# A new written-out order for the first 28 slices of a fused attention and gated-FFN kernel, with one load moved and four copies split

## The chip, the cores and the metric

The kernel runs on one core of a Trainium2 chip. The metric is the device time of one execution in microseconds (us). The kernel before takes 221.94 us, the median of three runs (221.68 to 222.19). The five engines are TensorE (PE in the profile; PEld is its weight loading), VectorE (DVE), ScalarE (ACT), GpSimd (POOL) and SyncE (SP). Each takes its own instructions strictly in the order in which the kernel lists them, and waits for another engine through semaphores.

## The reference

Eight batches, eight heads, 512 tokens and 32 state rows of width 64. Tokens attend to the state and the state attends to the tokens; both results, 8 x 544 rows of 512 numbers, go through a gated feed-forward layer.

```
a      = softmax(scale * x @ state^T)        # tokens over state rows
xread  = a @ state
a2     = softmax(scale * state @ x^T)        # state rows over tokens
sread  = a2 @ x
X      = rows of concat([xread, sread])      # 4352 x 512
out    = (relu(X @ w_gate) * (X @ w_val)) @ w_out     # d_ff = 1536
```

The softmax's subtraction of the maximum and the 1e-9 are not in the kernel, whose inputs keep the scores small.

## The kernel before, in words

All matmul operands are bf16. `xread @ w_gate` is regrouped as `a @ (state @ w_gate)`: for each batch the kernel first makes U, the product of the batch's state with both weight matrices, and then multiplies the transposed attention weights `ans` by U. Work is cut into **slices**: slice (b, jf) is 128 of the 1536 hidden columns of batch b. A step has a short name, and these names are used throughout:

- `gv.b.jf` (L289): four matmuls of 128x512 that make gate and value of a slice in two PSUM banks. `re` (L313) is ScalarE's ReLU of the gate bank, `mu` (L317) VectorE's product of it with the value bank. A bank is free once its reader (`re` for the first of the two banks, `mu` for the second) is done.
- `o.b.i` (L326): four output matmuls, a third of one 128-token block; `of` (L334, `fin_x`) copies a finished block out of PSUM on ScalarE and stores it from SP's queue.
- `c` and `co` (L262, L284): U of batches 0 and 1 in pieces of 128 or 256 columns as the weights arrive, and its copy out of PSUM; `u` and `uo` (L262, L274): the same for later batches, 512 columns at a time.
- `dx`, `dw`, `do`, `ds`: loads of x, of the two first weight matrices, of `wo` and of the state, all issued by GpSimd, one after the other. `xc` and `stc` convert to bf16 what came in as f32.
- `stT`/`sto`, `xT`/`xo`, `aT`/`ao`: transposes on TensorE of the state, of x and of the attention weights, each with its copy out of PSUM; `xd` (L148), `ad` (L197) and `state_T_dma` (L122): the same by a DMA transpose from SP's queue, with `state_out_dma` (L130) as GpSimd's copy of the state into its place.
- `sc`, `ex`, `nr`, `nx`: scores (L170), exponential on ScalarE (L177), row sums and reciprocal (L183, L185) and scaling (L189) on VectorE.
- `xp` (`x_pad`, L224): GpSimd copies x into a padded buffer, of which there are two, taken in turn; `sr` (L232) and `sn` (L241): the state's attention over tokens from that buffer, and its scaling.
- `spin`: a matmul on zeros whose result nobody reads; `on`: a memset of the padding.

The order is set in three parts. First come some direct statements (x of batch 0, the state of batches 0 and 1, the identity, memsets). Then a string, `program`, lists every step of the first 28 slices (batches 0 and 1, and slices 0 to 3 of batch 2) word by word; `@30` behind a step gives the PSUM banks it takes, and `.act`, `.dve` or `.pool` the engine of a copy. The last loop makes the slices from (2, 4) on: in each turn `gv`, `re`, `mu`, one `o` piece that lags by 18 slices, and then the units that `at(b, jf, ...)` hung on this slice: `att_half` (the `sc ex nr nx` of the next batch), `u_block` (three `u` with their copies), `sr`, `x_trans_dma`, `x_pad`, `x_load`. In that loop `bank` deals out the six banks 0 to 5 in turn to `gv`, `sc` and `u`, and 6 and 7 to the `o` blocks.

The scheduler is in manual mode: nothing is reordered between the text and the engines' queues, except that loads of weights run ahead of matmuls on TensorE.

Of the kernel before, what the change touches and what calls it, by code (L numbers as in the profile page):

```python
# [16 lines left out]
def kernel(  # L17
# [9 lines left out]
    nc = tc.nc  # L27

    B, H, S, D = x.shape
# [26 lines left out]
    HK = H // NK  # L56
# [12 lines left out]
    stT = const.tile([128, B, H, 64], BF16, name="stT")  # L69
# [6 lines left out]
    xf, xb, xT, e_sn, a_sn, ANS, U, hsb, sr_sb = {}, {}, {}, {}, {}, {}, {}, {}, {}  # L76
    copy = {"act": nc.scalar.copy, "dve": nc.vector.tensor_copy, "pool": nc.gpsimd.tensor_copy}

    given, turn = [], {"r": 0, "o": 1}

    def bank(name, kind="r"):

        if given:
            n = given.pop(0)
        elif kind == "spare":
            n = 6 + turn["o"] % 2
        else:
            n = turn["r"] % 6 if kind == "r" else 6 + turn["o"] % 2
            turn[kind] += 1
        return psum.tile([128, 512], FP32, name=name, tag=f"b{n}")  # L90

# [22 lines left out]
    def state_T(g):  # L114
        ps = held["st", g] = bank("stT_ps").bitcast(BF16)[:, 0:512]
        for i in range(4):
            nc.tensor.transpose(ps.rearrange("p (q i m) -> p q i m", i=4, m=8)[:, :, i],
                                st_b[:, g % 3, i].rearrange("p h d -> p (h d)"), id128)
# [31 lines left out]
    def x_T(b, lo, n):  # L150

        if b not in xT:
            xT_alloc(b)
        ps = held["xT", b, lo] = bank("xT_ps").bitcast(BF16)[:, 0:128 * n].rearrange("p (k t) -> p k t", t=128)
        for k in range(n):
            nc.tensor.transpose(ps[:, k], x_blocks(b)[:, lo + k], id128)  # L156
# [5 lines left out]
    def att_sc(b, jp):  # L162
        if b not in e_sn:
            e_sn[b] = att.tile([128, 2, NC, NJ * Ns], BF16, name="e_sn", tag="e_sn", bufs=4)
            a_sn[b] = att.tile([128, 2, NC, NJ * Ns], BF16, name="a_sn", tag="a_sn")
        t = held["sc", b, jp] = bank("sc_ps")
        ps = t.rearrange("p (r c j n) -> p r c j n", r=2, c=NC, j=2)
        for h in range(4 * jp, 4 * jp + 4):
            for k in range(2):
                nc.tensor.matmul(ps[:, h % 2, 2 * k:2 * k + 2, h // 2 % 2], xT[b][:, 2 * h + k], stT[:, b, h],  # L170
                                 start=True, stop=True)
# [49 lines left out]
    def x_pad(b):  # L221

        v = xa[:, b % NX].rearrange("p (c h) d -> p h c d", c=NC)[:, :, :, 0:D]
        nc.gpsimd.tensor_copy(out=v, in_=xb[b])  # L224

    def sr_mm(b, kind="r"):

# [170 lines left out]
    def spin(n, cols=512):  # L398
        for i in range(n):
# [6 lines left out]
             "sc": att_sc, "ex": att_exp, "nr": att_sum, "nx": att_scale, "aT2": att_T2, "ao2": att_out2, "aT": att_T, "ao": att_out,  # L406
             "c": c_unit, "co": c_out, "u": u_unit, "uo": u_out, "gv": gv, "re": relu, "mu": mult, "o": out_part,
             "of": fin_x, "xd": x_trans_dma, "ad": att_aT_dma, "xp": x_pad, "sr": sr_mm, "sn": sr_norm}
    program = """
    dx.1.0.2 dx.1.1.2 stc.0.0.act stc.0.1.act xc.0.0.dve dw.0.0.128 spin.7 stT.0@4 xc.0.1.act dw.1.0.128 on xT.0.0.4@2  # L410
    sto.0.0.dve sto.0.1.act xT.0.4.4@5 xo.0.0.4.dve dw.0.128.128 xo.0.4.4.dve dw.1.128.128 spin.1 sc.0.0@3 dw.0.256.256 ex.0.0 xT.0.8.4@0
    xT.0.12.4@1 xo.0.8.4.dve dw.1.256.256 xo.0.12.4.act nr.0.0 spin.2 sc.0.1@6 dw.0.512.256 xT.1.0.8@4 ex.0.1 nx.0.0
    xo.1.0.8.act nr.0.1 dw.1.512.256 spin.2 xT.1.8.8@2 xo.1.8.8.dve sc.1.0@5 dw.0.768.256 ex.1.0 nx.0.1 dw.1.768.256
    spin.2 c.0.0.128@30 sc.1.1@1 co.0.0.128.0.act nr.1.0 aT.0.1@6 co.0.0.128.1.act dw.0.1024.256 aT.0.0@4 ex.1.1
    ao.0.0.dve ao.0.1.act dw.1.1024.256 spin.1 c.0.128.128@25 c.1.0.128@30 nr.1.1 co.0.128.128.1.act gv.0.0@14
    co.0.128.128.0.act co.1.0.128.1.act nx.1.0 re.0.0 dw.0.1280.256 c.1.128.128@65 nx.1.1 gv.0.1@20 co.1.0.128.0.act
    co.1.128.128.0.act mu.0.0 co.1.128.128.1.act aT.1.1@7 re.0.1 dw.1.1280.256 aT.1.0@1 ao.1.1.act c.0.256.256@36
    ao.1.0.dve c.1.256.256@54 mu.0.1 co.0.256.256.0.act gv.1.1@21 dx.2.0.1 co.1.256.256.0.act co.0.256.256.1.dve
    re.1.1 gv.1.0@73 co.1.256.256.1.act mu.1.1 ds re.1.0 c.1.512.256@05 c.0.512.256@62 co.1.512.256.1.dve
    co.1.512.256.0.act gv.1.2@41 co.0.512.256.1.act mu.1.0 do.0.6 co.0.512.256.0.act gv.0.3@70 re.1.2 xp.1 gv.1.5@52  # L420
    re.0.3 mu.1.2 re.1.5 mu.0.3 gv.0.4@36 mu.1.5 re.0.4 xp.0 c.1.768.256@47 c.0.768.256@15 mu.0.4 co.1.768.256.0.act
    gv.0.2@03 co.0.768.256.0.act co.1.768.256.1.dve re.0.2 gv.0.5@26 do.6.12 co.0.768.256.1.act mu.0.2 gv.1.7@41 dx.3.0.1
    re.0.5 re.1.7 mu.0.5 gv.0.7@70 mu.1.7 re.0.7 gv.1.3@53 mu.0.7 re.1.3 gv.1.4@24 mu.1.3 re.1.4 gv.1.6@61 mu.1.4
    re.1.6 c.1.1280.256@70 c.0.1280.256@53 mu.1.6 co.1.1280.256.0.act c.1.1024.256@24 stc.1.0.pool xT.2.0.8@6
    co.0.1280.256.0.act co.1.1024.256.0.dve xT.2.8.8@1 co.0.1280.256.1.act co.1.1024.256.1.dve stc.1.1.pool
    c.0.1024.256@75 xo.2.8.8.act gv.0.10@23 co.1.1280.256.1.dve stc.3.1.pool co.0.1024.256.1.dve re.0.10 gv.1.9@40
    co.0.1024.256.0.act xo.2.0.8.dve stc.2.0.pool re.1.9 gv.0.6@12 mu.0.10 stc.3.0.pool re.0.6 mu.1.9 gv.0.11@57 mu.0.6
    stc.2.1.pool re.0.11 gv.0.8@64 mu.0.11 re.0.8 stT.1@3 gv.1.10@10 mu.0.8 sto.1.0.act sto.1.1.dve re.1.10 sc.2.0@2 o.0.0@7 ex.2.0
    mu.1.10 nr.2.0 sc.2.1@5 gv.0.9@34 ex.2.1 re.0.9 nx.2.0 o.0.1 mu.0.9 gv.1.11@12 nr.2.1 xd.3 re.1.11 o.0.2 mu.1.11
    o.0.3@6 nx.2.1 ad.2 of.0.0.act u.2.0.1024@05 u.2.1.512@34 uo.2.0.1024.0.dve uo.2.0.1024.1.act sr.0@1 sr.1@2  # L430
    uo.2.1.512.1.act sn.0 u.2.0.0@50 sn.1 xp.2 xp.3 o.0.4 uo.2.0.0.0.act uo.2.0.0.1.dve uo.2.1.512.0.dve
    o.0.5 o.0.6@7 of.0.1.act u.2.1.0@12 u.2.0.512@50 uo.2.1.0.0.act uo.2.1.0.1.dve u.2.1.1024@34 o.0.7
    uo.2.1.1024.0.act uo.2.1.1024.1.dve uo.2.0.512.0.act gv.1.8@12 uo.2.0.512.1.dve re.1.8 o.0.8 mu.1.8
    o.0.9@6 of.0.2.act gv.2.0@45 re.2.0 gv.2.2@01 mu.2.0 re.2.2 gv.2.1@23 mu.2.2 re.2.1 gv.2.3@45 mu.2.1
    re.2.3 mu.2.3
    """
    for word in program.split():
        word, _, banks = word.partition("@")
# [8 lines left out]
    def at(b, jf, f, *args):  # L447
        units.setdefault(NF * b + jf, []).append(lambda: f(*args))
# [20 lines left out]
        sr_norm(b)  # L469

    first, lag = 2 * NF + 4, 18
    at(2, 6, x_load, 4, 0, 1)
    for g in (2, 3):
        at(2, 2 + g, state_T_dma, g)
        at(2, 8 + g, state_out_dma, g, 0, "pool")
        at(2, 8 + g, state_out_dma, g, 1, "pool")
    for b in range(3, B):
        s = b - 1
        for i, jf in enumerate((4, 5) if b == 3 else (3, 4)):
            at(s, jf, att_half, b, i)  # L480
        for part, jf in enumerate((7, 10)):
            at(s, jf, u_block, b, part)
            paired.add(NF * s + jf)
        if b + 1 < B:
            at(s, 9, x_trans_dma, b + 1)
            at(s, 9, x_pad, b + 1)
        if b + 2 < B:
            at(s, 10, x_load, b + 2, 0, 1)
# [7 lines left out]
    for g in range(first, NF * (B + 1)):  # L496
        b, jf = divmod(g, NF)
# [47 lines left out]
```

## Time and profile before

| what | value |
|---|---|
| median of 3 runs | 221.94 us (221.68 to 222.19) |
| the profiled execution, its own time | 222.66 us |
| its span, from the first to the last instruction | 220.9 us |
| mean granted TensorE clock | 0.999 |
| busy: PE, DVE, ACT, POOL | 214.6, 130.8, 123.5, 40.6 us |
| gv (L289) and o (L326) matmuls | 94.1 and 94.6 us busy |
| GpSimd's idle time ahead of the padding copies (L224) | 69.2 us, of it 52.2 for `sr` on TensorE |

A busy PE in the page is not a PE at its peak, because the ends of pipelined matmuls are modelled; the start of each instruction says more. In the second part of the page each digit is a fortieth of the span (5.5 us). The timeline view gives for each engine the start of an instruction (or of a run of equal ones), its length, the number behind `x`, and in brackets the idle time just before it with the instruction or transfer that ended it.

### The profile page before, as it was taken

To read this page: it belongs to the slowest core of one execution; us is meant where nothing else is said; L and a number is where in the kernel's file an instruction comes from. 1 tells how busy PE (TensorE), PEld (TensorE's weight loads), DVE (VectorE), ACT (ScalarE), POOL (GpSimd) and SP (SyncE) were. 2 spreads that over 40 slices of the span, in tenths; PEclk is the share of its full clock that TensorE was granted. 3 is DMA by queue.
4 is the path that set the end of the run, shared out by engine and by line. 5 is a ranking of instruction groups with operands and counts; after the bars stand their busy time and mean duration, and the time that the engine had idled before them with its cause. 6 is when DMAs were issued, how large, how long until landed. Compare 5 with 4: busy or idle time off the path is not lost.

```text
span 220.9 us, 4858 instructions
## 1 busy us (share of the span) xinstructions
PE 214.6 (97%) x1955; PEld 105.2 (48%) x1955; DVE 130.8 (59%) x229; ACT 123.5 (56%) x236; POOL 40.6 (18%) x51
## 2 busy tenths in 40 slices
PE   7899999999999999999999999999999999999994
PEld 2553454444544444444444444445454445666543
DVE  5796898865787567664766487648665334222100
ACT  4699887465666565555566555646654543223221
POOL 7875830080035400040003000000000000000000
PEclk9999999999999999999999999999999999999999
DMA  7999999579057993655353105501411122222132
GB/s 165 165 195 197 198 241 204 52 213 167 8 127 112 185 142 98 142 96 103 85 130 83 50 19 142 121 16 43 112 37 53 47 47 50 50 57 85 50 95 96
DMA packets 42215, 23.65 MB, mean 107 GB/s; under 512 B 22640, under 2 KB 37872, under 8 KB 42192
## 3 DMA queue, kind: packets, MB, share of 16 engines
q0 software_dynamic: 16896, 9.05, 30.4%
q1 hardware_dynamic: 24400, 13.54, 24.3%
q10 hardware_dynamic: 896, 0.75, 1.4%
q8 instruction: 15, 0.25, 0.5%
q14 instruction: 8, 0.07, 0.1%
HBM read 18.35 MB, written 8.91 MB: 123 GB/s over the span
## 4 chain that ended last, share of the span: by engine, by line
PE 89%; DMA 7%; issue 1%; DVE 1%; POOL 1%; POOLq 0%
PE o_ps L326 39%; PE gv_ps L289 36%; PE gv_ps L306 5%; PE up L262 4%; DMA wv_sb<-in_moe_w_val_dram 4%; DMA xb<-in_x_dram 3%; PE sc_ps L170 1%; PE sr_ps L232 1%; PE o_ps L355 1%; PE upc L262 1%; PE xT_ps L156 0%; POOL xb L394 0%; DVE h_sb L317 0%; DVE stT L134 0%; POOL id masks.py:199 0%
## 5 line engine op out<-in xcount | busy, mean ns | idle before, releaser
L326 PE MATMUL o_ps<-wo_sb,h_sb 128*128 128x512 bf16 x372 | 94.6, 380 | 0.0
L289 PE MATMUL gv_ps<-ans,U 128*128 128x512 bf16 x384 | 94.1, 380 | 0.0
L317 DVE TENSOR_TENSOR h_sb<-gv_ps,g_sb 128x512 bf16<-128x512 f32 x96 | 65.3, 689 | 45.2 <-ACT g_sb L313 44.1
L313 ACT ACTIVATE g_sb<-gv_ps 128x512 bf16<-128x512 f32 (+1 forms) x108 | 63.0, 586 | 44.9 <-PE gv_ps L289 33.8
L289 PEld LDWEIGHTS <-U 128*128 128x128 bf16 x384 | 36.3, 98 | 42.2 <-issue 0.4
L326 PEld LDWEIGHTS <-h_sb 128*128 128x128 bf16 x372 | 35.3, 98 | 40.8 <-issue 2.1
L224 POOL COPY xa<-xb 128x2048 bf16<-128x2048 bf16 x8 | 15.1, 1898 | 69.2 <-PE sr_ps L232 52.2
L334 ACT COPY o_sb<-o_ps 128x512 f32<-128x512 f32 x31 | 18.3, 590 | 16.8 <-PE o_ps L326 14.8
L274 DVE CAST U<-up 128x512 bf16<-128x512 f32 x36 | 22.7, 685 | 5.7 <-PE up L262 5.6
L274 ACT CAST U<-up 128x512 bf16<-128x512 f32 x36 | 18.9, 594 | 12.1 <-PE up L262 12.0
L177 ACT ACTIVATE e_sn<-sc_ps 128x512 bf16<-128x512 f32 x16 | 9.6, 599 | 10.6 <-PE sc_ps L170 10.6
L317 DVE TENSOR_TENSOR hs_sb<-gv_ps,g_sb 128x256 bf16<-128x256 f32 x12 | 5.1, 425 | 15.1 <-PE gv_ps L306 9.2
L183 DVE TENSOR_REDUCE cs<-e_sn 128x16 f32<-128x512 bf16 x16 | 10.9, 681 | 4.4 <-ACT e_sn L177 4.4
L189 DVE TENSOR_TENSOR a_sn<-e_sn,rc 128x512 bf16<-128x512 bf16 x16 | 10.9, 686 | 0.4
L262 PEld LDWEIGHTS <-stT 64*32 64x32 bf16 x560 | 6.3, 90 | 9.6 <-issue 8.3
L284 ACT CAST U<-upc 128x512 bf16<-128x512 f32 (+1 forms) x21 | 10.0, 551 | 1.1 <-PE upc L262 1.1
L170 PEld LDWEIGHTS <-xT 128*128 128x128 bf16 x128 | 5.8, 98 | 4.4 <-issue 0.9
L262 PE MATMUL up<-wg_sb,stT 64*32 64x512 bf16 (+1 forms) x168 | 7.3, 349 | 0.0
L262 PE MATMUL up<-wv_sb,stT 64*32 64x512 bf16 (+1 forms) x168 | 7.3, 349 | 0.0
L170 PE MATMUL sc_ps<-stT,xT 128*128 128x64 bf16 x128 | 6.7, 193 | 0.5 <-DVE stT L134 0.3
L306 PE MATMUL gv_ps<-br,wg_sb 128*128 128x256 bf16 x48 | 7.2, 273 | 0.0
L306 PE MATMUL gv_ps<-br,wv_sb 128*128 128x256 bf16 x48 | 7.2, 273 | 0.0
(54 smaller groups left out, 112.9 us busy)
## 6 DMA issues: line engine op xcount, KB each, us to landing
out_dram<-o_sb SPq DMA_DIRECT2D x26, 256.0 KB, 2.4
xb<-in_x_dram POOLq DMA_DIRECT2D x6, 512.0 KB, 7.1
wo_sb<-in_moe_w_out_dram POOLq DMA_DIRECT2D x2, 768.0 KB, 13.5
out_dram<-o_sb SPq DMA_DIRECT2D x11, 128.0 KB, 2.4
wg_sb<-in_moe_w_gate_dram POOLq DMA_DIRECT2D x5, 256.0 KB, 9.4
wv_sb<-in_moe_w_val_dram POOLq DMA_DIRECT2D x5, 256.0 KB, 10.0
xb<-in_x_dram POOLq DMA_DIRECT2D x3, 256.0 KB, 5.9
st_f<-in_state_dram POOLq DMA_DIRECT2D x1, 384.0 KB, 11.5
```

Source lines behind the costliest of these rows:

```text
L170: nc.tensor.matmul(ps[:, h % 2, 2 * k:2 * k + 2, h // 2 % 2], xT[b][:, 2 * h + k], stT[:, b, h], start=True, stop=True)
L183: nc.vector.reduce_sum(out=cs, in_=e_v, axis=AX.X)
L189: {"dve": nc.vector, "pool": nc.gpsimd}[eng].tensor_tensor(out=by_pair(a_sn[b], jp).rearrange("p r (j n) -> p r j n", n=Ns), in0=e_v, in1= ...
L224: nc.gpsimd.tensor_copy(out=v, in_=xb[b])
L262: nc.tensor.matmul(dst[parity][32 * j:32 * j + 32], stT[r:r + 64, b, 2 * j + parity, 32 * parity:32 * parity + 32], wsb[r:r + 64, j, lo:lo ...
L274: copy[eng](out=U[b][:, w, kc, lo:lo + 512], in_=held["u", b, w, lo][kc])
L289: nc.tensor.matmul(ps[w], U[b][:, w, kc, f0:f0 + 128], ANS[b][:, kc].rearrange("p c t -> p (c t)"), start=(kc == 0), stop=(kc == NK - 1))
L306: nc.tensor.matmul(ps[w][:, 0:nt], wsb[:, j, f0:f0 + 128], br[:, j].rearrange("p b n -> p (b n)"), start=(j == 0), stop=(j == NJ - 1))
L313: nc.scalar.activation(out=g_sb[:, 0:n], in_=ps[0][:, 0:n], func=AF.Relu)
L317: nc.vector.tensor_tensor(out=dst, in0=ps[1][:, 0:n], in1=held["g", b, jf][:, 0:n], op=ALU.mult)
L326: nc.tensor.matmul(held["o", b, tsub], src[:, jf, tsub * 128:(tsub + 1) * 128], wo_sb[:, jf], start=(jf == 0), stop=(jf == NF - 1))
L334: copy[eng](out=o_sb, in_=held["o", b, tsub])
```

## The change

1. The `program` string is another list. Steps, engines of the copies and banks are chosen anew; all steps that compute something appear as before. There are 18 `spin` matmuls in place of 15. The state comes ahead of x at the start, `sc.1.0` comes behind both transposes of x of batch 1, `gv.0.0` comes behind four `c` units in place of three; x of batch 3 is loaded behind a cast of the state, and `xp.3` stands before `xp.2`. The list ends otherwise: `gv.2.1 gv.2.3 gv.2.0`, three `o`, then `gv.2.2`, and the `re` and `mu` of three of the four slices behind it.
2. `bank` deals out banks 1, 0, 4, 2, 3, 5 in the last loop in place of 0 to 5, and begins the `o` banks with the other one.
3. `x_pad` makes two copies of four heads each in place of one of eight.
4. x of batch 4 is loaded at slice (2, 5) behind `state_out_dma` of state group 2 (batches 4 and 5), which moves from slice (2, 10) to (2, 5); it was at (2, 6), with nothing of the state ahead of it. The copies for group 3 stay at (2, 11).

```diff
-    given, turn = [], {"r": 0, "o": 1}
+    given, turn = [], {"r": 0, "o": 0}
...
-            n = turn["r"] % 6 if kind == "r" else 6 + turn["o"] % 2
+            n = (1, 0, 4, 2, 3, 5)[turn["r"] % 6] if kind == "r" else 6 + turn["o"] % 2
...
-        nc.gpsimd.tensor_copy(out=v, in_=xb[b])
+        for hs in (slice(0, HK), slice(HK, H)):
+            nc.gpsimd.tensor_copy(out=v[:, hs], in_=xb[b][:, hs])
...
     program = """
...
+    stc.0.0.dve stc.0.1.act spin.7 stT.0@0 sto.0.1.dve dx.1.0.2 dx.1.1.2 dw.0.0.128 xc.0.1.dve dw.1.0.128
+    dw.0.128.128 dw.1.128.128 dw.0.256.256 dw.1.256.256 dw.0.512.256 dw.1.512.256 dw.0.768.256 dw.1.768.256
+    dw.0.1024.256 dw.1.1024.256 dw.0.1280.256 dw.1.1280.256 dx.2.0.1 ds xc.0.0.act on xp.0 xT.0.0.4@1 do.0.6
+    xT.0.4.4@2 sto.0.0.act xo.0.0.4.dve xo.0.4.4.act spin.3 sc.0.0@3 xT.0.8.4@4 xT.0.12.4@5 ex.0.0 xo.0.12.4.act
+    xo.0.8.4.dve nr.0.0 spin.3 sc.0.1@6 xT.1.0.8@0 xT.1.8.8@1 ex.0.1 nx.0.0 xo.1.0.8.act spin.2 sc.1.0@2
+    c.1.0.128@34 c.0.0.128@56 nr.0.1 xo.1.8.8.dve spin.1 sc.1.1@0 nx.0.1 ex.1.0 co.0.0.128.0.act aT.0.1@1 aT.0.0@2
+    ex.1.1 co.1.0.128.0.act ao.0.0.act c.1.128.128@50 spin.2 c.0.128.128@32 nr.1.0 co.0.0.128.1.act
+    co.0.128.128.0.act co.0.128.128.1.act ao.0.1.dve gv.0.0@16 co.1.128.128.1.act re.0.0 xp.1 co.1.0.128.1.act
...
+    c.1.256.256@57 co.0.256.256.1.act ao.1.1.dve co.1.256.256.0.dve mu.0.1 mu.0.0 co.1.256.256.1.act gv.1.1@20
...
+    mu.0.3 gv.1.5@20 stc.1.0.pool mu.1.0 mu.0.2 re.1.5 gv.0.5@34 re.0.5 mu.1.5 c.0.768.256@67 c.1.768.256@52 mu.0.5
+    stc.1.1.pool stc.2.0.pool c.0.1024.256@13 do.6.12 co.0.768.256.0.act co.1.768.256.0.dve gv.0.4@04
...
+    co.1.1280.256.1.dve co.0.1280.256.0.act re.1.6 co.1.1024.256.1.act re.0.7 gv.1.11@42 stT.1@1 xT.2.0.8@0
+    gv.0.9@35 sto.1.0.dve xo.2.0.8.dve mu.0.7 mu.1.6 sto.1.1.act re.1.11 re.0.9 xT.2.8.8@1 gv.1.10@40 re.1.10
...
+    mu.1.9 mu.1.8 nr.2.1 nx.2.1 o.0.5 u.2.1.512@10 u.2.1.0@54 u.2.0.0@23 uo.2.1.512.1.act o.0.1 uo.2.1.0.0.dve
+    uo.2.1.512.0.dve uo.2.0.0.1.dve ad.2 of.0.1.act o.0.2 u.2.0.1024@06 uo.2.0.0.0.act uo.2.1.0.1.act u.2.1.1024@52
+    u.2.0.512@14 of.0.0.act sr.1@3 sr.0@7 uo.2.0.1024.1.dve sn.1 sn.0 uo.2.0.512.1.dve uo.2.0.512.0.act o.0.6@6
+    uo.2.1.1024.1.dve stc.3.0.pool dx.3.0.1 stc.2.1.pool xd.3 xp.3 uo.2.0.1024.0.act xp.2 stc.3.1.pool gv.2.1@13
+    gv.2.3@07 gv.2.0@42 o.0.7 re.2.3 mu.2.3 o.0.8 of.0.2.act o.0.9@7 gv.2.2@06 re.2.1 re.2.2 re.2.0 mu.2.0 mu.2.2
+    mu.2.1 uo.2.1.1024.0.dve
     """
...
-    at(2, 6, x_load, 4, 0, 1)
     for g in (2, 3):
         at(2, 2 + g, state_T_dma, g)
-        at(2, 8 + g, state_out_dma, g, 0, "pool")
-        at(2, 8 + g, state_out_dma, g, 1, "pool")
+    for half in range(2):
+        at(2, 5, state_out_dma, 2, half, "pool")
+        at(2, 11, state_out_dma, 3, half, "pool")
+    at(2, 5, x_load, 4, 0, 1)
```

In the changed kernel the lines behind `x_pad` stand one lower, and those of the last loop up to three lower. The prediction uses the line numbers of the kernel before.

## The prediction

> **What bounds the kernel now.** I read the page's busy row, then the chain of work that ended last, then the timelines of the first 60 us.
>
> ```profile
> PE 214.6 (97%) x1955; PEld 105.2 (48%) x1955; DVE 130.8 (59%) x229; ACT 123.5 (56%) x236; POOL 40.6 (18%) x51
> ...
> PE 89%; DMA 7%; issue 1%; DVE 1%; POOL 1%; POOLq 0%
> ```
>
> TensorE is the bound, and its useful work is the same in both kernels. So the change can only alter what TensorE loses: the wait before the first slice, and single waits after it. The timeline of TensorE, VectorE and ScalarE shows the first kind; the slice work (L289) begins at 13.19 us:
>
> ```profile
> 9.96 0.62 PE L156 MATMUL xT_ps<-id,xb 128*128 128x128 bf16 x8 [0.28 <-DMA xb<-in_x_dram]
> ...
> 10.62 0.69 DVE L159 COPY xT<-xT_ps 128x1024 bf16<-128x1024 bf16 x1 [0.48 <-PE xT_ps L156]
> ...
> 11.23 0.68 DVE L189 TENSOR_TENSOR a_sn<-e_sn,rc 128x512 bf16<-128x512 bf16 x1
> ...
> 12.76 0.61 ACT L219 COPY ans<-aT_ps 128x512 bf16<-128x512 bf16 x1
> ...
> 13.19 1.04 PE L289 MATMUL gv_ps<-ans,U 128*128 128x512 bf16 x4
> ```
>
> The second kind is small. Between 13 and 60 us only two waits of TensorE exceed 0.3 us, one for weights at 19 us and one for the state at 37 us:
>
> ```profile
> 19.00 0.30 PE L262 MATMUL upc<-wv_sb,stT 64*32 64x256 bf16 x8 [0.46 <-DMA wv_sb<-in_moe_w_val_dram]
> ...
> 37.77 0.39 PE L170 MATMUL sc_ps<-stT,xT 128*128 128x64 bf16 x8 [0.35 <-DVE stT L134]
> ```
>
> Last, VectorE's own timeline where the written-out order ends. It is idle 0.84 us, and then has no gap until 63.34 (62.06 + 1.28):
>
> ```profile
> 56.71 0.69 DVE L317 TENSOR_TENSOR h_sb<-gv_ps,g_sb 128x512 bf16<-128x512 f32 x1 [0.17 <-ACT g_sb L313]
> 58.23 0.69 DVE L183 TENSOR_REDUCE cs<-e_sn 128x16 f32<-128x512 bf16 x1 [0.84 <-ACT e_sn L177]
> 58.96 0.25 DVE L185 RECIPROCAL rc<-cs 128x16 f32<-128x16 f32 x1
> 59.24 0.69 DVE L189 TENSOR_TENSOR a_sn<-e_sn,rc 128x512 bf16<-128x512 bf16 x1
> 59.85 0.68 DVE L317 TENSOR_TENSOR h_sb<-gv_ps,g_sb 128x512 bf16<-128x512 f32 x1
> 60.45 0.68 DVE L183 TENSOR_REDUCE cs<-e_sn 128x16 f32<-128x512 bf16 x1
> 61.17 0.25 DVE L185 RECIPROCAL rc<-cs 128x16 f32<-128x16 f32 x1
> 61.46 0.69 DVE L189 TENSOR_TENSOR a_sn<-e_sn,rc 128x512 bf16<-128x512 bf16 x1
> 62.06 1.28 DVE L317 TENSOR_TENSOR h_sb<-gv_ps,g_sb 128x512 bf16<-128x512 f32 x2
> 63.42 1.89 DVE L274 CAST U<-up 128x512 bf16<-128x512 f32 x3
> ```
>
> The third `u` unit of batch 3 takes the bank that the last of these multiplies (`mu.2.7`, done at 63.34) frees, and TensorE's rows put that unit at 63.35. So in this place VectorE and TensorE are level, with nothing to spare.
>
> **Unit prices, from the timelines.** A slice or an `o`: 0.865 us (20 matmuls in 4.32). `re` starts 0.63 behind its slice (51.99 to 52.62), takes 0.60, and follows another at 0.54 (two in 1.14). `mu` starts 0.03 behind its `re`, takes 0.69, and follows another at 0.62 (four in 2.55). TensorE follows a release by 0.05. A `c` of two weights, 256 columns: 0.29 in a pair, 0.26 in a triple, with 0.10 ahead of the group. Eight transposes 0.46, eight `sc` 0.23, a `spin` 0.22 once the clock is up (at the start they are 0.42 apart).
>
> **The head.** State ahead of x moves `stT` from 4.45 to about 4.15, where the seven `spin` end, but both pieces of x still land at 4.34 and about 5.0, and their casts have changed engines. `sc.0.0` comes 0.1 later, `sc.0.1` 0.25 later. This costs nothing: `xT.1.8.8` still waits for its load until 9.96, the copy follows at 10.62, and `nx.0.1` ends at 11.91 as before. That load hides the six `spin` of this stretch; without it they would cost up to 6 x 0.22. Behind it two more `spin` and two `c` stand ahead of `sc.1.1` (11.86), so `ex.1.1` runs 12.30 to 12.90 on ScalarE. It frees a bank of `c.1.128.128` and holds back `co.1.0.128.0` (0.33), `ao.0.0` (0.61) and `co.0.0.128.1` (0.33), at 12.84, 13.14 and 13.70. `c.0.128.128` waits for `ao.0.0` until 13.80, and `gv.0.0` starts at 14.15 in place of 13.19, with one `c` more behind it (0.25).
>
> **From there to 25 blocks (`gv` or `o`).** Before, 25 blocks are done at 41.68 (24 would be `gv` but for 1.8). In the new order they need: 25 x 0.865 = 21.62; ten `c` in two pairs and two triples, 2 x 0.58 + 2 x 0.78 + 4 x 0.10 = 3.12; `aT.1` 0.46; `xT.2` 1.00; `stT` 0.22; two `sc` 0.46; together 26.88. I followed each bank and each copy through the list and found only waits of 0.05 to 0.1 us, so I add 0.12: 14.15 + 27.0 = **41.15, 0.53 ahead**. Both waits of before go. That of 0.46 goes because TensorE comes to `dw.1.512` at 18.9 to 19.0, when it lands; what is late next there is `dw.1.1024`. The queue moved 2432 KB from 18.97 to the state's landing at 30.84, 205 KB/us, so it lands near 24.0, and TensorE wants it at 24.6. The 0.65 at 37 us goes because `stT.1` runs at 32.65, with a slice and a transpose ahead of its use; its casts follow the landing at 30.84 and end at 31.6.
>
> **To the end of the list.** From there the list holds 13 blocks (11.25), six `u` and two `sr` in both. The before takes 13.77 (41.68 to 55.45); with fewer changes between groups I make it 13.6 now, so TensorE would be at slice (2, 4) at 54.77, **0.68 ahead**. `ad.2` follows `nx.2.1` (45.05) and lands 3.1 later (all but one of the six; one took 4.9), at 48.2; `gv.2.1` wants it at 48.7.
>
> **What this end of the list costs.** `gv.2.2` starts at T = 53.9. ScalarE has `of.0.2`, `re.2.1`, `re.2.2`, `re.2.0` in this order, so `re.2.0` starts at T + 0.63 + 0.54 and ends at T + 1.78, though its slice is long done. VectorE, idle for some 4 us, now has four operations at once: `mu.2.0`, `mu.2.2`, `mu.2.1`, `uo.2.1.1024.0` at T + 1.81 and each 0.61 later. TensorE goes on with `gv.2.4`, `o.0.10` and `sc.3.0` to T + 2.82, and the second half of `gv.2.5` (T + 3.27) takes bank 3 from `mu.2.1`, which ends at T + 3.74: a wait of 0.5. `mu.2.4` starts at T + 4.25, `nr.3.0` at T + 4.86 = 58.76, 0.53 later than the row at 58.23. From there VectorE has no gap, so `mu.2.7` ends at 63.87, and the third `u` unit starts at 63.92 in place of 63.35. TensorE's lead of 0.68 has become a lag of 0.5 to 0.6. Behind 66 us VectorE has gaps again and TensorE none, so the lag stays to the end.
>
> **The other edits, at nothing.** *Copies in halves*: by a cast of 256 elements at 0.40 and a copy of 2048 at 1.90 a half is about 1.05 (an estimate from these two rows), 0.2 more a batch; GpSimd was idle 69.2 us ahead of these copies. Without that cover 0.2 us a batch for `sr`. *GpSimd's queue at the start*: `on` and `xp.0` delay `do.0.6` from 20.58 to 22.9, and three casts that wait for the state delay `do.6.12` from 25.13 to about 32. The first half of `wo` occupies the queue to 34.5, so the second lands at 38.3 to 39.5 and `dx.3` at 41 to 42; their first users stand at 41.15 (`o.0.4`) and 56.5 (`sc.3.0`). *x of batch 4* goes from 48.32 to about 59.7: it is queued behind `xp.2`, and behind copies that wait for a DMA transpose issued near 54.4 that lands 2.5 to 4.1 later, and two copies of 0.61. It lands near 67.7; `xd` on SP's queue took it at 67.86, its transpose 8.0, and `sc.4` is due near 79. *Banks and the other `o` bank* move no work.
>
> **Sum.** Made against the profiled execution: 222.66 + 0.55 = 223.2. That execution lies 0.72 above the median shown, whose 221.94 becomes **222.5 us**. A measurement of this kernel can tell about 0.2% (0.44 us) from no change.
>
> **The rivals.**
> 1. *The backlog on VectorE costs nothing*, because its four operations run faster or TensorE meets no occupied bank. Then the lead of 0.68 stays: 221.3, faster. For it: TensorE is the bound of the page as a whole. Against it: the banks, and the row at 63.35. Chance 0.12.
> 2. *Lead and backlog cancel*: T falls about 0.5 earlier (13.4 is the earliest for `gv.0.0` if the ScalarE row of four copies shrinks by 0.6), and the lag is the T of the day minus 53.35: 221.8 to 222.2. Chance 0.20.
> 3. *The lag is larger*, by one more wait within the list: ScalarE's row at 12.3 to 14.1 is the place, the price the time by which `ao.0.0` ends after 13.75, and it decides from 0.4 on: 222.9 to 223.6. `dw.1.1024` (0.6 to spare) and `ad.2` (0.5 to spare; 1.3 late at its worst landing of 4.9) would add in the same way. Chance 0.12.
> 4. *GpSimd's copies hold VectorE.* They now run near 58 to 59.7, where VectorE has no gap and `nx.3.0` stands at 59.8. In the before GpSimd is idle from 49.2 to 64.3, so no row shows the two side by side; one such wait is at least nothing and at most a copy of 0.61: 222.5 to 223.1. Chance 0.06. The Trainium skill, "SBUF — State Buffer", section "SBUF: two separate sides", says that VectorE and GpSimd share a port pair as an exclusive lock, which a VectorE operation with two SBUF inputs (`nx` is one, `mu` with its PSUM input is not) can wait on for the whole of a GpSimd copy. By that rule the sum would be 223.1 if they overlap; no row of the before can confirm it.
>
> **Chances.** Forecast 0.50 (222.2 to 222.9, a tenth of it below 222.38), rivals as above. Faster than 221.50: 0.12. Within 0.2%: rival 2 and the forecast's lower part, 0.30. Slower: 0.58. The range for 8 in 10 leaves out most of rival 1 and the upper part of rivals 3 and 4: 221.4 to 223.4.
>
> **What would show it.** In the changed profile: the first L289 matmul near 14.15; no wait of TensorE for `wv_sb` at 19 or for `stT` at 37; then a wait of TensorE for VectorE's multiply (now L318) near 57 to 58, VectorE without a gap from about 55.7 to 64, and `u` of batch 3 at 62.9 to 64 waiting for it. The prediction is wrong if VectorE has a gap between 58 and 63, or if a load or `ad.2` holds TensorE.

## The result, and the profile after

The changed kernel takes **222.79 us** (median of 22 runs, 221.72 to 223.75), the kernel before 221.94 (22 runs, 221.65 to 222.90): ratio 1.0032, 95% interval 1.0017 to 1.0048. It is slower by about 0.7 us by the ratio and 0.85 by the medians.

The one profiled execution of each says the opposite: 222.02 us after (span 220.2) against 222.66 before (span 220.9). The profiled execution of the changed kernel is one of its quickest, that of the kernel before one of its slower ones. So the two traces can't simply be set against each other. I cut each trace at four points that all kernels of this study have and compared the pieces, with a second trace of the kernel before (run e10_before, 221.73 us) and a second one of the changed kernel (run e4_again, 223.33 us). All in us:

| stretch | before | e10_before | after | e4_again |
|---|---|---|---|---|
| start to the first `gv` matmul | 13.19 | 12.80 | 13.68 | 14.98 |
| first `gv` to `o.0.10` | 43.12 | 42.54 | 41.40 | 41.40 |
| `o.0.10` to `sr` of batch 2 | 7.42 | 7.43 | 8.50 | 8.50 |
| from there to the last output matmuls | 151.10 | 151.09 | 151.10 | 151.09 |
| from there to the end of the span | 6.04 | 6.06 | 5.56 | 5.55 |

`o.0.10` is the first `o` behind slice (2, 4), and `sr` of batch 2 follows the first three `u` units of batch 3. Against e10_before, the changed kernel loses 0.88 at the head, gains 1.14 in the middle of the list, loses 1.07 at the end of the list and gains 0.50 at the very end: +0.31 in all. (In the second row the first trace of before is the odd one: e2_moves, e5_halves and e6_x4, which have its list, show 42.46 to 42.73.) The rest I put down to what e4_again shows against the first trace of the changed kernel: a head of 14.98 in place of 13.68, and nothing else that differs. Of the kernel's 34 times, 15 lie above 222.9 (10 of the 22 above, 5 of 12 of e4_again). That line is not sharp: the nearest times are 222.87 and 223.03, and the two sides have means of 222.27 and 223.35. The clear gap is in e3_list, which has the same list: three of its ten times are at 222.24 to 222.42, seven at 223.27 to 224.05. If all 15 are executions with the late head, of which one has a trace, they add 15/34 x 1.30 = 0.57 to the mean. 0.31 + 0.57 = 0.88 is an estimate from four traces; the medians differ by 0.85, the means by 0.71.

The page of the changed kernel, the rows of busy time and of the chain that ended last:

```profile
PE 211.9 (96%) x1929; PEld 105.8 (48%) x1958; DVE 132.7 (60%) x235; ACT 120.5 (55%) x230; POOL 41.8 (19%) x59
...
PE 88%; DVE 3%; issue 3%; DMA 3%; POOL 1%; ACT 1%; DVEq 0%; POOLq 0%
```

TensorE still bounds the kernel. The share of loads in the chain fell from 7% to 3%, that of VectorE rose from 1% to 3%: waits for transfers went, waits for VectorE came.

The head, in the timeline of all engines of the changed kernel (start, length, then the instruction):

```profile
9.61 0.62 PE L156 MATMUL xT_ps<-id,xb 128*128 128x128 bf16 x8 [0.39 <-DMA xb<-in_x_dram]
...
10.49 0.63 DVE L159 COPY xT<-xT_ps 128x1024 bf16<-128x1024 bf16 x1
...
11.03 0.68 DVE L189 TENSOR_TENSOR a_sn<-e_sn,rc 128x512 bf16<-128x512 bf16 x1
...
12.77 0.60 ACT L219 COPY ans<-aT_ps 128x512 bf16<-128x512 bf16 x1
...
13.68 1.90 PE L290 MATMUL gv_ps<-ans,U 128*128 128x512 bf16 x8
```

x of batch 1 came 0.35 earlier than in the first trace of before (9.61 to 9.96), yet the first slice starts 0.49 later, because more work stands ahead of it.

The end of the list on TensorE, from its timeline:

```profile
53.35 1.89 PE L290 MATMUL gv_ps<-ans,U 128*128 128x512 bf16 x8
55.08 1.03 PE L327 MATMUL o_ps<-wo_sb,h_sb 128*128 128x512 bf16 x4
...
57.04 0.38 PE L290 MATMUL gv_ps<-ans,U 128*128 128x512 bf16 x1 [0.27 <-DVE h_sb L318]
...
63.24 0.41 PE L263 MATMUL up<-wg_sb,stT 64*32 64x512 bf16 x7 [0.19 <-DVE h_sb L318]
63.58 0.44 PE L233 MATMUL sr_ps<-xa,e_sn 128*32 128x65 bf16 x32
```

And on VectorE:

```profile
55.10 1.89 DVE L318 TENSOR_TENSOR h_sb<-gv_ps,g_sb 128x512 bf16<-128x512 f32 x3 [4.11 <-ACT g_sb L314]
56.90 0.68 DVE L275 CAST U<-up 128x512 bf16<-128x512 f32 x1
...
58.10 0.67 DVE L183 TENSOR_REDUCE cs<-e_sn 128x16 f32<-128x512 bf16 x1
...
61.91 1.28 DVE L318 TENSOR_TENSOR h_sb<-gv_ps,g_sb 128x512 bf16<-128x512 f32 x2
```

VectorE is idle for 4.11 us, and then has four operations at once (three `mu` and `uo.2.1.1024.0` at 56.90). It has no gap from 55.10 to 63.2, and TensorE waits for its `mu` twice, at 57.04 and 63.24. This is the forecast backlog.

### The profile page after: what moved, and what is told of

The parts are those of the page before. It is cut to its first block, busy times and chain, and to the rows that moved or that the text cites. A ratio compares the mean times of both kernels' runs of the same rounds, so it can differ in the third digit from the quotient of the medians.

```text
span 220.2 us, 4833 instructions
## 1 busy us (share of the span) xinstructions
PE 211.9 (96%) x1929; PEld 105.8 (48%) x1958; DVE 132.7 (60%) x235; ACT 120.5 (55%) x230; POOL 41.8 (19%) x59
## 4 chain that ended last, share of the span: by engine, by line
PE 88%; DVE 3%; issue 3%; DMA 3%; POOL 1%; ACT 1%; DVEq 0%; POOLq 0%
PE o_ps L327 37%; PE gv_ps L290 35%; PE gv_ps L307 5%; PE up L263 4%; DMA xb<-in_x_dram 3%; DVE h_sb L318 2%; PE upc L263 2%; PE sc_ps L170 1%; PE sr_ps L233 1%; PE o_ps L356 1%; PE xT_ps L156 1%; DVE cs L183 1%; PE warm_ps L401 0%; POOL xb L395 0%; ACT g_sb L314 0%
## 5 line engine op out<-in xcount | busy, mean ns | idle before, releaser
L327 PE MATMUL o_ps<-wo_sb,h_sb 128*128 128x512 bf16 x356 | 91.2, 379 | 2.2 <-issue 1.7
L290 PE MATMUL gv_ps<-ans,U 128*128 128x512 bf16 x374 | 92.7, 379 | 0.5 <-DVE h_sb L318 0.3
L318 DVE TENSOR_TENSOR h_sb<-gv_ps,g_sb 128x512 bf16<-128x512 f32 x96 | 64.3, 688 | 45.1 <-ACT g_sb L314 44.3
L225 POOL COPY xa<-xb 128x1024 bf16<-128x1024 bf16 x16 | 16.3, 1051 | 62.9 <-PE sr_ps L233 58.0
L275 DVE CAST U<-up 128x512 bf16<-128x512 f32 x37 | 23.4, 684 | 3.6 <-PE up L263 3.6
L285 ACT CAST U<-upc 128x512 bf16<-128x512 f32 (+1 forms) x18 | 8.7, 514 | 1.2 <-PE upc L263 1.2
L401 PE MATMUL warm_ps<-hs_sb 128*128 128x512 bf16 x16 | 5.9, 488 | 1.4 <-DVE hs_sb L373 1.2
```

Of the source, the lines that this page charges most:

```text
L225: nc.gpsimd.tensor_copy(out=v[:, hs], in_=xb[b][:, hs])
L275: copy[eng](out=U[b][:, w, kc, lo:lo + 512], in_=held["u", b, w, lo][kc])
L290: nc.tensor.matmul(ps[w], U[b][:, w, kc, f0:f0 + 128], ANS[b][:, kc].rearrange("p c t -> p (c t)"), start=(kc == 0), stop=(kc == NK - 1))
L318: nc.vector.tensor_tensor(out=dst, in0=ps[1][:, 0:n], in1=held["g", b, jf][:, 0:n], op=ALU.mult)
L327: nc.tensor.matmul(held["o", b, tsub], src[:, jf, tsub * 128:(tsub + 1) * 128], wo_sb[:, jf], start=(jf == 0), stop=(jf == NF - 1))
```

## The experiments

The expectations set out their theories by letters. A is the prediction's: the end of the list costs the time, and the moved load and split copies nothing. B: the moved load and the split copies cost it. C: transfers that land later at the start cost it. Two were formed after the first four runs. D: the start of TensorE's full clock makes the group of longer times. E: a load of instructions near the end lengthens the last stretch. Ratios are to the kernel before in the same set of runs.

**e1_end: the end of the list reordered.** The changed kernel, with `re` and `mu` right behind their slices and the copy of `u` ahead of three `o`:

```diff
-    gv.2.3@07 gv.2.0@42 o.0.7 re.2.3 mu.2.3 o.0.8 of.0.2.act o.0.9@7 gv.2.2@06 re.2.1 re.2.2 re.2.0 mu.2.0 mu.2.2
-    mu.2.1 uo.2.1.1024.0.dve
+    gv.2.3@07 re.2.1 mu.2.1 gv.2.0@42 re.2.3 mu.2.3 re.2.0 mu.2.0 uo.2.1.1024.0.dve o.0.7 o.0.8 of.0.2.act o.0.9@7 gv.2.2@06 re.2.2 mu.2.2
```

> The changed kernel with only the end of its list put in another order: re.2.1, re.2.3, re.2.0 and their mu directly behind their slices, and uo.2.1.1024.0 behind mu.2.0, all ahead of o.0.7; the slices, the banks and TensorE's own order stay. Theory A (the four operations that VectorE gets at once at the end of the list hold TensorE at gv.2.5 and at the u units of batch 3): in the changed kernel's trace TensorE starts gv.2.4 at 54.2 against 55.45 before, and has only 0.15 of this lead left at sr of batch 2 (63.58 against 63.73), so about 1.0 to 1.1 us are lost there; this kernel gets them back, 0.9 to 1.2 us faster than the changed kernel and 0.1 to 0.5 us faster than the kernel before, and VectorE shows an idle gap ahead of nr.3.0. Theory B (the moved load and the split copies on GpSimd make the loss): no change against the changed kernel, about 0.7 us slower than before. Theory C (the start makes it, by transfers that land later in most executions): no change either.

Measured: 221.28 us (220.73 to 222.57, 12 runs), ratio 0.9964 (0.9943 to 0.9984). `o.0.10` to `sr` falls from 8.50 to 7.42, the value of the kernel before. VectorE's timeline of e1_end:

```profile
54.94 0.69 DVE L318 TENSOR_TENSOR h_sb<-gv_ps,g_sb 128x512 bf16<-128x512 f32 x1 [2.17 <-ACT g_sb L314]
55.80 0.69 DVE L318 TENSOR_TENSOR h_sb<-gv_ps,g_sb 128x512 bf16<-128x512 f32 x1 [0.17 <-ACT g_sb L314]
57.33 0.69 DVE L183 TENSOR_REDUCE cs<-e_sn 128x16 f32<-128x512 bf16 x1 [0.84 <-ACT e_sn L177]
...
61.16 1.28 DVE L318 TENSOR_TENSOR h_sb<-gv_ps,g_sb 128x512 bf16<-128x512 f32 x2
```

The gap of 0.84 ahead of `nr.3.0` is back, the same as in the kernel before. The last `mu` of the stretch ends at 62.44 in place of 63.19. One line of the order undone takes 1.08 from the stretch and makes the kernel faster than both, so A holds. The stretch hardly varies by itself: it is 7.42 or 7.43 in all eight traces with the old or the mended end, and 8.50 in all three with the changed one.

**e2_moves, e5_halves, e6_x4: the other parts alone**, each on the kernel before. e5 has the first of these edits, e6 the second, e2 both:

```diff
-        nc.gpsimd.tensor_copy(out=v, in_=xb[b])
+        for hs in (slice(0, HK), slice(HK, H)):
+            nc.gpsimd.tensor_copy(out=v[:, hs], in_=xb[b][:, hs])
...
-    at(2, 6, x_load, 4, 0, 1)
...
+        at(2, 5, state_out_dma, 2, half, "pool")
...
+    at(2, 5, x_load, 4, 0, 1)
```

> The kernel before with only parts 3 and 4 of the change: copies of the padded x in halves, the state copies of group 2 at slice (2, 5), and x of batch 4 loaded behind them. Theory A: within 0.2 us of the kernel before, since GpSimd has idle time and x of batch 4 is not due before 79 us. Theory B: slower by 0.5 to 0.9 us, with nx of batch 3 or an SP transpose held up near 58 to 68 us. Theory C: no change.

> The kernel before with part 3 alone, the padding copies in halves. Theory E (new): from the start of the last output matmuls (L355, L356 in the changed kernel) to the end of the span the kernel before takes 6.04 us and e3_list 5.94, but the changed kernel, e1_end, e2_moves and e4_again take 5.53 to 5.57; the two slower ones have a load of instructions at 220.9 and 221.8, the others none there. The eight added copies lengthen GpSimd's list, so its last load of instructions comes earlier: this kernel should end 5.5 to 5.6 us behind the start of the last matmuls. If the moved load of x makes it, 5.9 to 6.1.

> The kernel before with part 4 alone: state copies of group 2 at slice (2, 5), x of batch 4 behind them. Theory E: 5.9 to 6.1 us from the last matmuls' start to the end of the span, with a load of instructions near the end, and the same time as before everywhere else (7.42 from o.0.10 to sr of batch 2, 151.1 from there to the last matmuls). If part 4 shortens the end, 5.5 to 5.6.

Measured: e2_moves 221.52 us (221.13 to 222.95, 12 runs), ratio 0.9984 (0.9963 to 1.0004), which alone decides nothing, but excludes that these parts cost 0.7 us: B fell. Its trace has a last stretch of 5.57 in place of 6.04. Single executions part the two: e5_halves 221.54 us with 5.56, e6_x4 222.12 us with 6.07. So the split copies shorten the end by half a microsecond, and the moved load does nothing: its 151.09 is the value of every kernel. The transfers in the last 1.2 us of the span, from the view of DMA queues (packets, MB, share of 16 engines), of e6_x4:

```profile
DMA packets 1, 0.01 MB, mean 7 GB/s; under 512 B 0, under 2 KB 0, under 8 KB 0
...
q14 instruction: 1, 0.01, 2.2%
```

and of e5_halves:

```profile
DMA packets 0, 0.00 MB, mean 0 GB/s; under 512 B 0, under 2 KB 0, under 8 KB 0
```

What comes last in e6_x4 is a load of instructions on queue q14. All four traces that have one at the end (before, e10_before, e6_x4, e3_list) have a last stretch of 5.94 to 6.07. All others, whose last load on that queue is at 185 to 193 us, have one of 5.54 to 5.57. (Queue q8 has a later load, at 204 to 208 us, in all twelve.) So theory E told the two kinds apart, but the load at the end can't itself be the cause. By the trace's own records it starts within 0.02 us of the end of the span, and the time is lost ahead of it, on GpSimd: its closing instructions, which the timeline leaves out, go on with a DRAIN that starts 5.31 to 5.35 behind the start of the last output matmuls in these four traces and 4.97 to 4.98 in the other eight, and lasts 0.15 to 0.24 in place of 0.09 to 0.10. The split adds eight instructions to GpSimd. Why GpSimd then closes sooner, and why the load moves with it, stays open.

**e3_list and e4_again: the list without the other parts, and the changed kernel once more.** e3_list is the changed kernel with the edits above taken back; e4_again is unaltered.

> The changed kernel with parts 3 and 4 undone, so the new list and banks alone. Theory A: as slow as the changed kernel, 0.5 to 0.9 us slower than before. Theory B: as fast as before or faster, by up to 0.7 us. Theory C: as the changed kernel.

> The changed kernel unaltered, for a second trace and to see the others beside it on one chip; its 22 times so far lie between 221.72 and 223.75 and its one trace belongs to a fast execution (222.02), so one trace says too little of the median. All theories: 0.4 to 1.1 us slower than before. Theory A expects this trace too to lose about 1 us between gv.2.4 and sr of batch 2; theory C expects an execution with a time above 223 to show its loss ahead of 40 us instead, in a later landing of x of batch 1 or of the weights.

Measured: e3_list 223.59 us (222.24 to 224.05, 10 runs), ratio 1.0046 (1.0022 to 1.0069), with 8.50 at the end of the list and 5.94 at the very end; e4_again 222.62 (221.75 to 223.53, 12 runs), ratio 1.0015 (0.9994 to 1.0035). The list alone carries all the loss. Of the 0.97 between these two medians, the split copies explain the 0.4 at the very end (5.94 to 5.55); besides, seven of ten times of e3_list lie in its upper group, and five of twelve of e4_again. What no theory so far had named: both traces have a first slice at 14.93 to 14.98, 1.3 later than the first trace of the changed kernel. TensorE's timeline of e4_again and then of the changed kernel's first trace, at the same steps:

```profile
6.00 0.61 PE L156 MATMUL xT_ps<-id,xb 128*128 128x128 bf16 x4 [0.38 <-DVE xb L138]
6.41 1.49 PE L401 MATMUL warm_ps<-hs_sb 128*128 128x512 bf16 x3
7.68 0.63 PE L170 MATMUL sc_ps<-stT,xT 128*128 128x64 bf16 x8
```

```profile
5.95 0.40 PE L156 MATMUL xT_ps<-id,xb 128*128 128x128 bf16 x4 [0.57 <-DVE xb L138]
6.19 0.81 PE L401 MATMUL warm_ps<-hs_sb 128*128 128x512 bf16 x3
6.83 0.48 PE L170 MATMUL sc_ps<-stT,xT 128*128 128x64 bf16 x8
```

Three `spin` take 1.49 in place of 0.81, and every step behind them comes later: TensorE is at half speed here, and it waits for no load in this trace, so theory C doesn't explain it. The trace's first record of the full clock is at 9.72 in e4_again and at 4.65 in the other. (The page's PEclk row doesn't show this; it reads 9 from the first slice on. The lengths of the matmuls do.) This is theory D.

**e8_uo: one step moved.** The changed kernel, only with `uo.2.1.1024.0.dve` ahead of `o.0.7`:

```diff
-    gv.2.3@07 gv.2.0@42 o.0.7 re.2.3 ...
-    mu.2.1 uo.2.1.1024.0.dve
+    gv.2.3@07 gv.2.0@42 uo.2.1.1024.0.dve o.0.7 re.2.3 ...
+    mu.2.1
```

> The changed kernel with one copy moved: uo.2.1.1024.0 ahead of o.0.7, so that VectorE has three operations at the end of the list in place of four. Theory A, with 0.60 us for one operation in VectorE's row: TensorE still waits for mu.2.1 at gv.2.5, but the u units of batch 3 start 0.60 earlier, so from o.0.10 to sr of batch 2 TensorE needs 7.9 in place of 8.50 us (7.42 before). If it is ScalarE's late re alone that counts, 8.50 stays.

Measured, one execution: 222.28 us, and 7.90 from `o.0.10` to `sr`, 0.60 less than 8.50. VectorE's timeline:

```profile
55.93 2.48 DVE L318 TENSOR_TENSOR h_sb<-gv_ps,g_sb 128x512 bf16<-128x512 f32 x4 [4.11 <-ACT g_sb L314]
58.34 0.68 DVE L183 TENSOR_REDUCE cs<-e_sn 128x16 f32<-128x512 bf16 x1
```

The four `mu` now follow each other without the copy between them. Taking one operation of the backlog away gives back one VectorE pitch (2.48 for four with a last one of 0.68: 0.60 each). Had the backlog been hidden, this would have given nothing.

**e9_few and e7_fill: the clock, provoked and cured.** Both are e1_end with other numbers of `spin`. e9_few has three fewer at the start:

```diff
-    stc.0.0.dve stc.0.1.act spin.7 stT.0@0 sto.0.1.dve ...
+    stc.0.0.dve stc.0.1.act spin.4 stT.0@0 sto.0.1.dve ...
```

> The kernel with the mended end (e1_end) and four spin ahead of the first transpose in place of seven, so that TensorE stands idle from about 2.9 to 4.4 us. Nothing that is waited for changes: the first transpose starts when the state's cast ends, at 4.43, in both. Theory D (TensorE's clock comes up after a stretch of about 3.4 us in which it was busy enough): it comes up late, at 8.5 to 10 us, in nearly all executions, so the first slice starts near 15.0, and the median rises by 0.8 to 1.3 us, to 222.1 to 222.6; the times of 220.7 to 221.3 go nearly all away. If the two groups of times have another cause (the landing of transfers): as e1_end, a median of 221.0 to 221.6.

Measured: 222.18 us (221.88 to 222.71, 10 runs), ratio 1.0006 (0.9991 to 1.0021). Compared with e1_end, work was removed and the time rose by 0.9. TensorE's timeline of e9_few:

```profile
1.19 1.89 PE L401 MATMUL warm_ps<-hs_sb 128*128 128x512 bf16 x4 [1.19 <-DVE hs_sb L373]
4.43 0.58 PE L117 MATMUL stT_ps<-id,st_b 128*128 128x128 bf16 x4 [1.35 <-DVE st_b L112]
...
6.39 1.49 PE L401 MATMUL warm_ps<-hs_sb 128*128 128x512 bf16 x3
...
8.96 1.49 PE L401 MATMUL warm_ps<-hs_sb 128*128 128x512 bf16 x3
...
15.38 0.82 PE L290 MATMUL gv_ps<-ans,U 128*128 128x512 bf16 x3
```

Behind the gap of 1.35, `spin` stays at half speed until 10.4 and the first slice starts at 15.38. None of the ten times is below 221.88, where e1_end has 9 of 12. D holds in this direction. The trace, of an execution of 222.63, is one of four at 222.59 to 222.71; how the start goes in the six at 221.88 to 222.26 isn't known. e7_fill adds three:

```diff
-    stc.0.0.dve stc.0.1.act spin.7 stT.0@0 sto.0.1.dve ...
+    stc.0.0.dve stc.0.1.act spin.8 stT.0@0 spin.1 sto.0.1.dve ...
...
-    ... xT.0.0.4@1 do.0.6
+    ... xT.0.0.4@1 spin.1 do.0.6
```

> The kernel with the mended end (e1_end) and three more spin in the first 6 us, where TensorE stood idle: spin.8 for spin.7, one behind stT.0 and one behind xT.0.0.4. Theory D (new; it joins theory A): the two groups of times that every kernel shows come from TensorE's clock. In the trace of the changed kernel a spin after 6 us took 0.22 and the first slice started at 13.68; in the second trace of the same kernel three spin at 6.41 took 0.43 each, and the first slice started at 14.98, with everything behind it as before. The changed start leaves TensorE idle for longer before 6 us, so the clock comes up one window late in more executions (15 of 34 times of the changed kernel above 222.9). With TensorE kept busy the clock should come up by 6 us in nearly all executions: at most 2 of 12 times more than 1 us above the fastest (the mended kernel has 3 of 12, the changed one 15 of 34), a median of 220.8 to 221.2 (221.28 without), the fastest as without. If the groups come from the landing of transfers, the share stays at a quarter to a half and the median does not move.

Measured: 221.27 us (220.87 to 221.93, 12 runs), ratio 0.9968 (0.9957 to 0.9980). In its trace the spins fill the gaps between the transposes:

```profile
5.00 0.63 PE L401 MATMUL warm_ps<-hs_sb 128*128 128x512 bf16 x1
...
5.85 0.43 PE L401 MATMUL warm_ps<-hs_sb 128*128 128x512 bf16 x1
```

No upper group shows: the twelve times lie within 1.06, where e1_end has three of twelve at 222.38 to 222.57. Three of twelve to none alone could be chance, but the three kernels with this start and fewer `spin` (the changed one, e1_end, e3_list) have 25 of 56 times in their upper groups. The median is no lower than e1_end's 221.28, though, against my expectation; the first slice comes at 13.61 by its trace, so the added spins cost the quick executions nothing that shows there. e7_fill is the best version by its times: the median of e1_end, and no upper group.

**e10_before: the kernel before, once more.**

> The kernel before unaltered, for a second trace of it: the one shown belongs to an execution of 222.66, 0.7 above its median. Expected: 7.42 to 7.43 us from o.0.10 to sr of batch 2 and a tail of 5.9 to 6.1 with a load of instructions near the end again (theories A and E), and a first slice between 12.5 and 13.3 with a time that follows it.

Measured, one execution: 221.73 us; the stretches are in the first table. Its clock comes at 6.65, later than in the changed kernel's quick trace, and yet the first slice starts at 12.80, so its head has room for that. Over all sets of runs the kernel before has 3 of 85 times from 222.9 up, the changed kernel 15 of 34. None of the five traces with the old list has a late clock; whether that start is spared it, or hides it, isn't shown.

## Why the prediction was right, point by point

The forecast of 222.5 missed the median by 0.3 us, and the main mechanism holds. But two terms that I had not seen came in with opposite signs, so part of the agreement is luck.

- **The backlog on VectorE** (0.68 lost and 0.53 of lag, 1.21): 1.08 measured, shown by e1_end and e8_uo. The wait on the second half of `gv.2.5`, forecast at 0.5, is 0.44 (56.60 to 57.04). Rival 1, that it costs nothing, is refuted.
- **The middle of the list**: from the first slice to T, the start of `gv.2.2`, I counted 39.75 and the trace has 39.67. The waits for weights and for the state are gone. In e8_uo a wait of 0.58 for the weights stands in this stretch (42.16 in place of 41.40), so such a wait depends on when a transfer lands, and can come back.
- **The head**: the first slice at 14.15 was forecast; 13.68 measured with the clock up early, mostly because x of batch 1 came at 9.61 and not 9.96, and 14.98 with the clock up late. The failed step is "That load hides the six `spin` of this stretch". It does at 0.22 a `spin`; at 0.43 each, `sc.0.1` starts at 9.99, behind the time at which the load had landed in the other trace. I had read the clock from the single trace of before, where it was up at 5.23, and taken it for a constant. That is rival 3's size by another mechanism: not ScalarE's row, but TensorE's clock.
- **The end of the kernel**, not in the sum: 0.5 gained, by the split copies that I put at nothing. The price of a half (1.05) was right, its cover too; GpSimd's closing instructions, where the time is gained, were not in the working.
- **From one execution to the median**: the walk came 0.68 early at the third `u` unit (63.24 for 63.92) and the end 0.5 early, together 1.2, and the profiled execution is indeed 222.02 for 223.2. I then took off 0.72, as if the changed kernel's median lay below its trace as that of before did. It lies 0.77 above. The 0.72 was no constant of the measurement: between before's two traces 0.97 arises ahead of `o.0.10` (56.31 to 55.34), in just the part that the change rewrites. Errors of -1.2 and +1.5 left 0.3.
- **Rival 2** (lead and backlog cancel, 221.8 to 222.2) describes the quick group nearly (222.02 in its trace), but not for its reason: 0.5 of it is the end of the kernel.
- **Rival 4**: GpSimd's copies ran from 56.22 to 57.50, earlier than I had them, beside three `mu` and a cast; `nx.3.0` came at 59.09 and took its usual 0.69. The rule of the Trainium skill, "SBUF — State Buffer", section "SBUF: two separate sides", speaks of VectorE operations with two SBUF inputs; none met these copies, so no run here tests it.
- **x of batch 4** went to 57.44 (59.7 forecast), and cost nothing, as forecast.
- **Slips in the working**, none of which moves the forecast: 41.15 + 13.6 is 54.75, not 54.77; the "0.65 at 37 us" is 0.35 of idle time in the row shown; and "a tenth of it" stands for 0.10, a fifth of the forecast's 0.50.

## What to carry to other kernels

On an engine that waits for its inputs in order, put each consumer right behind its producer: four steps held back to the end of a hand-written list cost TensorE 1.08 us up to 10 us later, though VectorE is busy only 60% of the time. When TensorE's start is rearranged, keep it free of gaps until its clock is up, and take several traces, because one start can be lucky. Where a change of 0.3% is judged, compare stretches between points that both kernels share, not whole spans.

## What the runs showed of the hardware

**The clock at the start.** By the trace's own records TensorE's full clock came at 3.90 to 6.65 us in nine traces, and at 9.63, 9.72 and 10.56 in e3_list, e4_again and e9_few. `spin` then runs every 0.22 in place of 0.43. In the changed kernel the first slice starts at 13.68 with an early clock and at 14.98 with a late one, 1.30 apart; e1_end, with the same start, an early clock and x of batch 1 at 9.95, has 14.01, which leaves 0.97. The same program shows both clocks (4.65 and 9.72). The full clock lasts 211.63, 215.04 or 218.45 us by these records, steps of 3.41.

The Trainium skill, "TensorE: Matmul & The Clock Gate", section "What's actually happening", says that TensorE begins at half rate and goes to the full one after a busy window of about 3.4 us, and that these windows run freely, whatever the kernel does. The traces agree with it: two levels, steps of 3.41, and a start that differs between executions of one program. As an estimate with the Trainium skill's 3.41 us, which is also the step above, and with each `spin` and transpose counted with its distance to the next at half rate (0.43 and about 0.1): windows that ended at 6.31 in e4_again and 7.15 in e9_few, with 71% and 60%, were not enough; those that ended at 6.65 in e10_before and 3.90 in e8_uo, with 78% and 80%, were. By the busy times of the profile, whose ends are modelled, the order isn't kept (86% and 67% against 89% and 79%), so these shares are no limit to build on. The Trainium skill adds in the same section that this start is less than 1% of a typical kernel; here its 1.30 us is 0.6%, and larger than the whole change.

**Loading of instructions.** A single transfer of 0.01 MB as the last thing of the run goes with 0.4 to 0.5 us at the end (5.94 to 6.07 against 5.54 to 5.57), while TensorE, VectorE and ScalarE have the same timeline up to there. It starts behind the lost time, which stands on GpSimd, so it marks the slower end and doesn't make it.
